# State-token block: first layer in three fp32r passes, low parts and convolution reordered, last stores cut in four

## The chip, the cores and the metric

One core of one Trainium2 chip runs the whole kernel. The metric is device time in microseconds (us) of one execution. The time before is the median of three runs, 946.2 us (944.11, 946.2 and 946.27).

## The reference, cut to what matters

Three layers follow one another. An attention reads `x` (8 batches, 8 heads, 512 tokens, 64 wide) against 32 state tokens and back, so that each batch has 512 + 32 tokens of width 512. Then a normalised two-layer block with a residual, then a gated causal convolution:

```python
xn = (x - mu) / np.sqrt(var + 1e-06) * g_ln
x  = x + np.maximum(xn @ w_ch1, 0.0) @ w_ch2      # 512 -> 2048 -> 512

gate_pre = sum(conv_w[k] * xp[:, k:k + S, :] for k in range(5))   # xp: x padded by 4 tokens in front
gate = 1.0 / (1.0 + np.exp(-gate_pre))
out  = (gate * (x @ w_val)) @ w_out
```

All arithmetic is float32.

## The kernel before, in words

**Arithmetic.** A float32 product is mostly made of three fp32r passes: each operand is split into a high part (a copy rounded to fp32r, made on ScalarE) and a low part (source minus high, made on VectorE or GpSimd), and `mm3` (lines 76 to 79) adds high by low, low by high and high by high. In the profile, L77, L78 and L79 are these three matmuls, whoever calls them. `split_sb` (lines 72 to 74) makes the two parts: L73 is the high one, L74 the low one.

**Stages.** The 512 ordinary tokens of batches 0 to 7 go through the two-layer block as token blocks b = 0 to 7. The 8 x 32 = 256 state tokens of all batches form one more token block, b = B = 8 ("the state block" below). Its input is made by `sread_block_steps` while block 7 runs: `xc` is the centred input, `xn` (line 420) is `xc` times the norm's weight `g`. `segment` (lines 536 to 629) runs 16 hidden slices f of 128 units: layer 1 into a PSUM tile `h`, relu into `hid` (L580 ScalarE high part, L582 VectorE low part), and layer 2, which for slice f is issued one slice later (`second`, by `run_pending`), so that TensorE goes L1(f), L2(f-1), L1(f+1), L2(f). For the ordinary blocks layer 1 is `mm3`. For the state block it is a plain float32 matmul, L565: four of them (k) per slice, 256 columns each, with the decoded weight pairs `w1_0` to `w1_7` as the stationary operand.

**The last stage.** For each of the nine blocks i, `split_x2` splits the block's result `x2` into high (L642) and low (L646 VectorE for i = 0, L644 GpSimd otherwise), `gate_x2` makes the convolution (L656, then four taps L658 on VectorE, then the sigmoid L670), `val_steps` multiplies by `w_val` and by the gate (L691) and splits the product, and `out_steps` multiplies by `w_out`, copies from PSUM (L707) and stores: two token tiles in one transfer (L711) for i < B, one transfer of 128 rows for each of the two tiles of the state block (L709). On TensorE the order is val(0), val(1), out(0), val(2), out(1), and so on to out(8). Each val uses the same four accumulators acc0 to acc3, so val(1) cannot begin slice e before L691 has read slice e of val(0).

**What sets the order.** TensorE's order is written out by hand. On the other engines a planner orders the instructions by priority and by a simulated timeline, and the engine then takes them in that fixed order. `behind` (lines 440 to 446) adds an ordering to that plan without a wait: the instruction comes after a marked one on the same engine. `marks["dve"]` is the last L582 of `segment`, `marks["act"]` the last L580. Behind the state block, in the slots after each slice (`before_phase_b`), run the loads of x2 of blocks 0 and 1, the decode of `w_out` (raw data go into the tiles `w1_0` to `w1_3`, once layer 1 has finished with these), and split and convolution of block 0.

**Buffers.** The tags `m` (two buffers, used by `m_steps` before), `ahl` (two) and `big` (two) are shared. x2 of block 1 takes a `big` buffer when the one before it is free.

Of the kernel before, what the change touches and what calls it, by code (L numbers as in the profile page):

```python
# [9 lines left out]
F32 = mybir.dt.float32  # L10
F32R = mybir.dt.float32r
# [4 lines left out]
AF = mybir.ActivationFunctionType  # L16
ALU = mybir.AluOpType
# [4 lines left out]
P = 128  # L22
# [22 lines left out]
def tile_kernel(ctx: ExitStack, tc: tile.TileContext, xT, xk, stT, sn, w1, w2, wval, wout, convw, gln, ident, out):  # L45
# [9 lines left out]
    def sb(shape, dt, tag, bufs=1):  # L55
        cnt[0] += 1
        return main.tile(shape, dt, tag=tag, bufs=BUFS.get(tag, bufs), name=f"{tag}_{cnt[0]}")
# [23 lines left out]
    def at_prio(p):  # L81
        tc.cur_priority = p
# [323 lines left out]
    def sread_block_steps():  # L406
        xs = sb([P, KT, NTS], F32, "big")
        for k in range(KT):
            nc.sync.dma_start(out=xs[:, k].rearrange("p (b n) -> p b n", n=NS), in_=x1d[:, :, k, :].rearrange("b p n -> p b n"))
        yield  # L410
        mu = at_ps([P, NTS])
        for k in range(KT):
            nc.tensor.matmul(mu, lhsT=nmean.to_broadcast([P, P]), rhs=xs[:, k], start=k == 0, stop=k == KT - 1)
        xc = sb([P, KT, NTS], F32, "big")
        xn = sb([P, KT, NTS], F32, "ahl")
        for k in range(KT):
            nc.vector.tensor_tensor(xc[:, k], xs[:, k], mu, op=ALU.add)
        yield
        for k in range(KT):
            nc.scalar.activation(xn[:, k], xc[:, k], AF.Copy, scale=g_sb[:, k])  # L420
        xns[B] = xn
        x1s[B] = xs
        yield
        sq = [t2([P, 2, NTS]) for _ in range(2)]
        for i in range(2):
            nc.scalar.activation(sq[i], xc[:, 2 * i:2 * i + 2], AF.Square)
        nc.gpsimd.tensor_tensor(sq[0], sq[0], sq[1], op=ALU.add)
        rstd_of(B, [sq[0][:, 0], sq[0][:, 1]], NTS)
        yield
# [102 lines left out]

    cs_done = set()
    clock = [BASE]

    def segment(b, f0, f1, n, nxt, bg):
        accs = {}
        for f in range(f0, f1):
            base = clock[0]
            clock[0] += 1000  # L540
            at_prio(base - DLEAD)
            for _ in range(next(share[0], 0)):
                next(slots[0], None)
            q, cols = f // QF, slice((f % QF) * P, (f % QF + 1) * P)
            unit = (b, q + 1) if (q + 1) * QF < f1 else nxt
            fresh = b < B and unit is not None and unit[1] not in cs_done
            if b < B and unit is not None and f % QF == 1 and not fresh:
                at_prio(base - 1500)
                m_steps(*unit)
            at_prio(base - HLEAD)  # L550
            if f == 1 and 1 < b < B:
                x1_group(b)
            at_prio(base)
            h = ps(ps_mm, "mm", [P, n])
            if b < B:
                m = ms[b, q]
                for u in range(2):
                    if plain(b, f):
                        nc.tensor.matmul(h, lhsT=m[:, u, 0, cols], rhs=aTs[b][:, u], start=u == 0, stop=u == 1)
                        continue  # L560
                    ahl = ahls[b]
                    mm3(h, m[:, u, 0, cols], m[:, u, 1, cols], ahl[:, u, 0], ahl[:, u, 1], u == 0, u == 1)
            else:
                for k in range(KT):
                    nc.tensor.matmul(  # L565
                        h, lhsT=w1s[4 * q + k][:, cols], rhs=xns[b][:, k], start=k == 0, stop=k == KT - 1
                    )
            if fresh and f % QF == 3:
                at_prio(base - 1500)
                colsum(unit[1])  # L570
                m_steps(*unit)
            if f == 1 and 1 < b < B:
                x1_mean(b)
            if f == f1 - 1:
                at_prio(base + LATE)
                for _ in bg:
                    pass
            at_prio(base - HLEAD)
            hid = sb([P, 2, n], F32 if plain(b, f) else F32R, "hid")
            marks["act"] = nc.scalar.activation(hid[:, 0], h, AF.Relu)  # L580
            if not plain(b, f):
                marks["dve"] = nc.vector.scalar_tensor_tensor(  # L582
                    hid[:, 1], h, 0.0, hid[:, 0].bitcast(F32), op0=ALU.max, op1=ALU.subtract
                )
            at_prio(base + 200)
            run_pending()

            def second(f=f, hid=hid):
                rrow = rstd_row(b, n) if f == f1 - 1 else None
                for d in range(KT):  # L590
                    if f == f0:
                        accs[d] = ps(ps_acc, f"acc{d}", [P, n])
                    cols = slice(d * P, (d + 1) * P)
                    if plain(b, f):
                        nc.tensor.matmul(accs[d], lhsT=plain_w2[f][:, cols], rhs=hid[:, 0], start=f == f0, stop=f == f1 - 1)  # L595
                    else:
                        mm3(accs[d], w2s[f][:, 0, cols], w2s[f][:, 1, cols], hid[:, 0], hid[:, 1], f == f0, f == f1 - 1)
                    if f == f1 - 1:
                        x1 = x1s[b]
                        dst = x1[:, d, :]  # L600
                        if b == B:
                            xp = sb([P, B, PAD + NS], F32, f"w1_{4 + d}")
                            nc.gpsimd.tensor_copy(xp[:, :, :PAD], halos[0][:, d])
                            x2s[B].append(xp)
                            dst = xp[:, :, PAD:]
                        t = t2([P, n])
                        p = tc.cur_priority
                        at_prio(p - HLEAD)
                        marks["dve"] = nc.vector.tensor_tensor(t, accs[d], rrow, op=ALU.mult)
                        at_prio(p)  # L610
                        eng = nc.vector if b < 2 or b >= B - 1 else nc.gpsimd
                        eng.tensor_tensor(dst, grouped(b, t), grouped(b, x1[:, d, :]), op=ALU.add)
                if f == NF - 1 and b < B:
                    nc.sync.dma_start(out=x2d[b], in_=x1s[b])
                    if not halos:
                        halos.append(sb([P, KT, B, PAD], F32, "halo"))
                    nc.gpsimd.tensor_copy(halos[0][:, :, b, :], x1s[b][:, :, S - PAD:])

            pend[0] = second
            at_prio(base + 500)  # L620
            next(bg, None)
# [15 lines left out]
    def split_x2(i, k):  # L637
        n = ntok(i)
        hl = sb([P, 2, n], F32R, f"w2_{4 * (i % 2) + k}")
        src = x2s[i][:, k] if i < B else x2s[i][k][:, :, PAD:]  # L640
        hi, lo = grouped(i, hl[:, 0]), grouped(i, hl[:, 1])
        behind(nc.scalar.activation(hi, src, AF.Copy), "act")  # L642
        if i:
            nc.gpsimd.tensor_tensor(lo, src, hi.bitcast(F32), op=ALU.subtract)  # L644
        else:
            behind(nc.vector.tensor_tensor(lo, src, hi.bitcast(F32), op=ALU.subtract), "dve")  # L646
        x2hl.setdefault(i, []).append(hl)
# [24 lines left out]
    def x2_steps(i):  # L672
        if i > B:
            return
        for k in range(KT):
            split_x2(i, k)
            yield
            gate_x2(i, k)
            yield

    def val_steps(i):
        n = ntok(i)
        hls = x2hl.pop(i)
        gt = gates.pop(i)
        gvs[i] = []
        for e in range(KT):
            v = ps(ps_acc, f"acc{e}", [P, n])
            cols = slice(e * P, (e + 1) * P)
            for k in range(KT):
                mm3(v, wv[k][:, 0, cols], wv[k][:, 1, cols], hls[k][:, 0], hls[k][:, 1], k == 0, k == KT - 1)  # L690
            nc.vector.tensor_tensor(gt[:, e], gt[:, e], v, op=ALU.mult)  # L691
            hl = sb([P, 2, n], F32R, f"w2_{8 + 4 * (i % 2) + e}")
            split_sb(hl[:, 0], hl[:, 1], gt[:, e], nc.vector)
            gvs[i].append(hl)
            yield

    def out_steps(i):
        n = ntok(i)
        hls = gvs.pop(i)
        for t in range(n // P):  # L700
# [5 lines left out]
                ob = sb([P, 2, DM], F32, "hid", 2)  # L706
            nc.scalar.copy(ob[:, t % 2], o)  # L707
            if i == B:
                nc.sync.dma_start(out=out[4 * t:4 * t + 4, S:, :], in_=ob[:, t % 2])  # L709
            elif t % 2:  # L710
                nc.sync.dma_start(  # L711
                    out=out[i, (t - 1) * P:(t + 1) * P, :].rearrange("(u p) d -> p u d", p=P), in_=ob
                )
# [249 lines left out]
```

## Time and profile before

| | us |
|---|---|
| median of three runs | 946.2 |
| profiled execution, its own time | 944.02 |
| its span, first to last instruction | 942.2 |
| TensorE busy in the span | 911.7 (97%) |
| VectorE busy | 563.9 (60%) |
| ScalarE busy | 367.4 (39%) |
| GpSimd busy | 193.1 (20%) |
| granted TensorE clock, mean share of full | 0.992 |

The profiled execution lasted 944.02 us, of which 942.2 lie between its first and its last instruction. A start time in a timeline is us from the beginning of the span. A matmul's duration is longer than the step to the next one, because matmuls are pipelined: the step between starts is what a matmul costs. In the same way the step between back-to-back VectorE instructions is a little shorter than the duration of one. The state block lies from 687 to 744 us, the last stage from 744 to the end.

### The profile page before, as it was taken

How to read it: one execution, taken by the hardware profiler on the slowest of the kernel's cores; microseconds unless marked ns; L12 is line 12 of the kernel's file. 1: busy time of each engine (PE TensorE's matmuls, PEld its weight loads, DVE VectorE, ACT ScalarE, POOL GpSimd, SP SyncE). 2: the span in 40 equal slices, each digit the busy share in tenths (PEclk: the TensorE clock that was granted, in tenths of full speed). 3: DMA queues.
4: the chain of work that ended last, by engine and by line, in shares of the span. 5: the costliest groups of instructions: out<-in, count | busy, mean ns of one | idle time of the engine just before them, and what ended most of it. 6: DMA issues, size and time to landing. Idle time of an engine off the chain costs nothing.

```text
span 942.2 us, 12810 instructions
## 1 busy us (share of the span) xinstructions
PE 911.7 (97%) x5087; PEld 687.9 (73%) x5088; DVE 563.9 (60%) x972; ACT 367.4 (39%) x672; POOL 193.1 (20%) x167
## 2 busy tenths in 40 slices
PE   7979999999999999999999999999999989999996
PEld 2327666777777777777777777777888878888884
DVE  6887997575357472453436336242138899988830
ACT  4646654233144332332314233232125454655521
POOL 0000000012114521412411241142102243232100
PEclk9989999999999999999999999999999999999999
DMA  9832220022103111111100110110021212321112
GB/s 364 325 114 93 71 71 1 1 93 96 41 8 118 46 48 48 48 48 49 48 21 25 48 45 1 27 46 18 27 90 46 90 45 90 129 96 62 51 67 67
DMA packets 26548, 66.45 MB, mean 71 GB/s; under 512 B 10744, under 2 KB 12920, under 8 KB 22392
## 3 DMA queue, kind: packets, MB, share of 16 engines
q1 hardware_dynamic: 26056, 64.45, 19.2%
q10 hardware_dynamic: 432, 1.18, 0.3%
q8 instruction: 40, 0.66, 0.3%
q14 instruction: 20, 0.16, 0.1%
HBM read 47.80 MB, written 17.83 MB: 70 GB/s over the span
## 4 chain that ended last, share of the span: by engine, by line
PE 79%; DVE 14%; DMA 2%; ACT 2%; issue 1%; SPq 0%; ACTq 0%; DVEq 0%
PE acc L77 14%; PE acc L79 14%; PE acc L78 13%; PE mm L77 8%; PE mm L79 7%; PE mm L78 7%; PE at L138 3%; DVE ahl L658 3%; PE at L77 2%; PE at L79 2%; PE at L78 2%; PE mm L565 1%; PE acc L595 1%; DVE w L458 1%; DVE hid L582 1%
## 5 line engine op out<-in xcount | busy, mean ns | idle before, releaser
L582 DVE SCALAR_TENSOR_TENSOR hid<-mm,hid 128x512 fp32r<-128x512 f32 (+1 forms) x140 | 92.2, 658 | 223.6 <-ACT hid L580 223.4
L77 PE MATMUL acc<-hid,w 128*128 128x512 f32 (+1 forms) x560 | 215.7, 385 | 2.3 <-DVE hid L582 1.2
L79 PE MATMUL acc<-hid,w 128*128 128x512 f32 (+1 forms) x560 | 211.5, 378 | 0.0
L78 PE MATMUL acc<-hid,w 128*128 128x512 f32 (+1 forms) x560 | 211.2, 377 | 0.0
L580 ACT ACTIVATE hid<-mm 128x512 fp32r<-128x512 f32 (+2 forms) x144 | 82.4, 572 | 246.8 <-PE mm L79 226.8
L77 PEld LDWEIGHTS acc<-hid,w 128*128 128x128 f32 x560 | 105.3, 188 | 25.4 <-DVE hid L582 2.2
L79 PEld LDWEIGHTS acc<-hid,w 128*128 128x128 f32 x560 | 105.3, 188 | 20.0
L78 PEld LDWEIGHTS acc<-hid,w 128*128 128x128 f32 x560 | 105.4, 188 | 19.4
L74 POOL TENSOR_TENSOR m<-mb,m 128x512 fp32r<-128x512 f32 x48 | 65.5, 1379 | 202.0 <-ACT m L73 202.0
L77 PE MATMUL mm<-ahl,m 128*128 128x512 f32 x248 | 102.3, 413 | 0.0
L658 DVE SCALAR_TENSOR_TENSOR ahl<-big,cw,ahl 128x509 f32<-128x509 f32 (+3 forms) x128 | 99.4, 830 | 4.1 <-ACT ahl L656 3.7
L78 PE MATMUL mm<-ahl,m 128*128 128x512 f32 x248 | 96.8, 390 | 0.2 <-DVE m L74 0.2
L79 PE MATMUL mm<-ahl,m 128*128 128x512 f32 x248 | 96.9, 391 | 0.0
L77 PEld LDWEIGHTS mm<-ahl,m 128*128 128x128 f32 x248 | 46.5, 188 | 38.0 <-issue 30.0
L73 ACT ACTIVATE m<-mb 128x512 fp32r<-128x512 f32 x62 | 39.1, 630 | 89.8 <-DVE mb L144 89.7
L644 POOL TENSOR_TENSOR w<-big,w 128x512 fp32r<-128x512 f32 x28 | 44.2, 1605 | 82.0 <-ACT w L642 82.0
L144 DVE SCALAR_TENSOR_TENSOR mb<-cs,sbn,at 128x512 f32<-128x512 f32 x62 | 43.5, 742 | 28.3 <-PE at L138 28.3
L77 PE MATMUL acc<-w,raw 128*128 128x512 f32 (+1 forms) x144 | 54.6, 379 | 2.5 <-DVE ahl L691 2.5
L78 PE MATMUL acc<-w,raw 128*128 128x512 f32 (+1 forms) x144 | 54.4, 378 | 0.0
L79 PE MATMUL acc<-w,raw 128*128 128x512 f32 (+1 forms) x144 | 54.3, 377 | 0.0
L79 PEld LDWEIGHTS mm<-ahl,m 128*128 128x128 f32 x248 | 46.5, 188 | 10.1
L78 PEld LDWEIGHTS mm<-ahl,m 128*128 128x128 f32 x248 | 46.7, 188 | 8.5 <-DVE m L74 0.5
(172 smaller groups left out, 1353.3 us busy)
## 6 DMA issues: line engine op xcount, KB each, us to landing
raw<-in_w SPq DMA_DIRECT2D x16, 512.0 KB, 4.7
w<-in_w SPq DMA_DIRECT2D x16, 512.0 KB, 9.8
big<-in_xk SPq DMA_DIRECT2D x8, 1024.0 KB, 4.9
x2d<-x SPq DMA_DIRECT2D x8, 1024.0 KB, 3.8
big<-x2d SPq DMA_DIRECT2D x8, 1024.0 KB, 4.9
out<-hid SPq DMA_DIRECT2D x16, 512.0 KB, 2.8
big<-in_xT SPq DMA_DIRECT2D x7, 1024.0 KB, 4.8
raw<-in_wval SPq DMA_DIRECT2D x4, 512.0 KB, 3.5
```

What stands on the lines that cost most here:

```text
L73: nc.scalar.activation(hi, src, AF.Copy)
L74: eng.tensor_tensor(lo, src, hi.bitcast(F32), op=ALU.subtract)
L77: nc.tensor.matmul(acc, lhsT=wh, rhs=xl, start=first, stop=False)
L78: nc.tensor.matmul(acc, lhsT=wl, rhs=xh, start=False, stop=False)
L79: nc.tensor.matmul(acc, lhsT=wh, rhs=xh, start=False, stop=last)
L138: nc.tensor.matmul(mp[u][32 * p:32 * p + 32, :], lhsT=stg[r, p, :], rhs=w1s[4 * q + p][r], start=True, stop=True)
L144: a = nc.vector.scalar_tensor_tensor(mb, cs[:, q], sbn[:, u], mp[u], op0=ALU.mult, op1=ALU.add)
L458: a = nc.vector.tensor_scalar(h[:, :, 0, 1], h[:, :, 1, 1], 0x8000, 0x4000, op0=ALU.bitwise_and, op1=ALU.bitwise_or)
L580: marks["act"] = nc.scalar.activation(hid[:, 0], h, AF.Relu)
L582: marks["dve"] = nc.vector.scalar_tensor_tensor(hid[:, 1], h, 0.0, hid[:, 0].bitcast(F32), op0=ALU.max, op1=ALU.subtract)
L644: nc.gpsimd.tensor_tensor(lo, src, hi.bitcast(F32), op=ALU.subtract)
L658: t = nc.vector.scalar_tensor_tensor(g[:, j:], x[:, :n - j], cw_sb[:, k, PAD - j:TAPS - j], g[:, j:], op0=ALU.mult, op1=ALU.add)
```

## The change

1. The state block's layer 1 becomes three fp32r passes. `xn` gets a high and a low part, and a new function `split_w1` splits the weights for two hidden slices at a time, in `m` buffers, two slices ahead of their use.
2. The low part of x2 of block 1 goes from GpSimd to VectorE, behind the last marked VectorE instruction. For block 1 all four splits come ahead of all four convolutions.
3. In `val_steps` the low part of the product becomes the new mark `marks["dve"]`, so convolutions emitted later are ordered behind it (for all blocks below B).
4. Each of the two last stores (256 KB, 128 rows) becomes four stores of 32 rows, on SyncE's and ScalarE's queues in turn.

```diff
@@ sread_block_steps
-        xn = sb([P, KT, NTS], F32, "ahl")
+        xn = sb([P, 2, KT, NTS], F32R, "ahl")
@@
-            nc.scalar.activation(xn[:, k], xc[:, k], AF.Copy, scale=g_sb[:, k])
+            nc.scalar.activation(xn[:, 0, k], xc[:, k], AF.Copy, scale=g_sb[:, k])
+            nc.vector.scalar_tensor_tensor(
+                xn[:, 1, k], xc[:, k], g_sb[:, k], xn[:, 0, k].bitcast(F32), op0=ALU.mult, op1=ALU.subtract
+            )
@@
+    w1hl = {}
+
+    def split_w1(i):
+        hl = sb([P, 2, KT, 2 * P], F32R, "m")
+        q, c = i // 2, slice((i % 2) * 2 * P, (i % 2 + 1) * 2 * P)
+        for j in range(2):
+            w = w1s[2 * q + j, "pair"][:, :, c]
+            split_sb(hl[:, 0, 2 * j:2 * j + 2], hl[:, 1, 2 * j:2 * j + 2], w, nc.vector)
+        w1hl[i] = hl
@@ segment
             at_prio(base - HLEAD)
+            if b == B and f % 2 == 0:
+                if f == 0:
+                    split_w1(0)
+                if f + 2 < f1:
+                    split_w1(f // 2 + 1)
@@
+                wc = slice((f % 2) * P, (f % 2 + 1) * P)
+                w, xn = w1hl[f // 2], xns[b]
                 for k in range(KT):
-                    nc.tensor.matmul(
-                        h, lhsT=w1s[4 * q + k][:, cols], rhs=xns[b][:, k], start=k == 0, stop=k == KT - 1
-                    )
+                    mm3(h, w[:, 0, k, wc], w[:, 1, k, wc], xn[:, 0, k], xn[:, 1, k], k == 0, k == KT - 1)
@@ split_x2
-        if i:
+        if i > 1:
             nc.gpsimd.tensor_tensor(lo, src, hi.bitcast(F32), op=ALU.subtract)
@@ x2_steps
             split_x2(i, k)
             yield
-            gate_x2(i, k)
-            yield
+            if i != 1:
+                gate_x2(i, k)
+                yield
+        if i == 1:
+            for k in range(KT):
+                gate_x2(i, k)
+                yield
@@ val_steps
-            split_sb(hl[:, 0], hl[:, 1], gt[:, e], nc.vector)
+            nc.scalar.activation(hl[:, 0], gt[:, e], AF.Copy)
+            a = nc.vector.tensor_tensor(hl[:, 1], gt[:, e], hl[:, 0].bitcast(F32), op=ALU.subtract)
+            marks["dve"] = a
@@ out_steps
             if i == B:
-                nc.sync.dma_start(out=out[4 * t:4 * t + 4, S:, :], in_=ob[:, t % 2])
+                for j in range(4):
+                    eng = nc.scalar if j % 2 else nc.sync
+                    eng.dma_start(out=out[4 * t + j, S:, :], in_=ob[32 * j:32 * j + 32, t % 2])
```

## Rows read from the trace of the kernel before

**Rows 1.** The page: busy time, share of the span and instructions of each engine.
```profile
PE 911.7 (97%) x5087; PEld 687.9 (73%) x5088; DVE 563.9 (60%) x972; ACT 367.4 (39%) x672; POOL 193.1 (20%) x167
```
**Rows 2.** Busy time by stretch: one stretch, the state block's sum, the first last-stage stretch.
```profile
711.00:726.00 15.00, 15.00 (x96) 13.82 (x95) 12.02 (x20) 8.71 (x16) 2.26 (x2) 1.00 0.19 70
...
sum 56.60, PE 55.40 PEld 50.67 DVE 36.74 ACT 21.96 POOL 7.41; mean PE 13.85 PEld 12.67 DVE 9.19 ACT 5.49 POOL 1.85
...
743.80:766.00 22.20, 19.72 (x87) 15.69 (x86) 22.05 (x26) 9.97 (x18) 13.30 (x8) 1.00 0.14 48
```
**Rows 3.** The chain that ended last, 699 to 744 us: start, length, what.
```profile
699.30 1.73 PE mm L565 x8
702.46 1.73 PE mm L565 x8
...
712.83 3.51 DMA w<-in_wout
...
739.41 4.89 DMA big<-x2d
```
**Rows 4.** TensorE's timeline, layer 2 of one slice: two matmuls, nine steps apart.
```profile
701.10 0.28 PE L79 MATMUL acc<-hid,w 128*128 128x256 f32 x1
...
702.17 0.28 PE L79 MATMUL acc<-hid,w 128*128 128x256 f32 x1
```
**Rows 5.** TensorE's timeline: the layer-1 starts of three slices in a row.
```profile
724.42 1.89 PE L565 MATMUL mm<-ahl,w 128*128 128x256 f32 x8
...
728.11 1.89 PE L565 MATMUL mm<-ahl,w 128*128 128x256 f32 x8
...
732.48 1.89 PE L565 MATMUL mm<-ahl,w 128*128 128x256 f32 x8
```
**Rows 6.** TensorE's waits from 686 us to the end: total us, times, longest.
```profile
PE acc L77 <- DVE ahl L691: 2.5, 2, 1.5
PE acc L77 <- DVE hid L582: 1.2, 2, 0.9
```
**Rows 7.** VectorE's and GpSimd's timelines: convolution taps alone, and beside GpSimd's low parts.
```profile
731.07 2.32 DVE L658 SCALAR_TENSOR_TENSOR ahl<-big,cw,ahl 128x511 f32<-128x511 f32 x3 [0.18 <-ACT ahl L656]
...
745.60 1.55 DVE L658 SCALAR_TENSOR_TENSOR ahl<-big,cw,ahl 128x511 f32<-128x511 f32 x1
...
748.52 3.48 DVE L658 SCALAR_TENSOR_TENSOR ahl<-big,cw,ahl 128x511 f32<-128x511 f32 x2
...
745.03 6.41 POOL L644 TENSOR_TENSOR w<-big,w 128x512 fp32r<-128x512 f32 x4 [4.07 <-ACT w L642]
```
**Rows 8.** Groups by line and shape: the two halves of a split, 512 elements.
```profile
L73 ACT ACTIVATE m<-mb 128x512 fp32r<-128x512 f32 x62 | 39.1, 630 | 89.8 <-DVE mb L144 89.7
...
L74 DVE TENSOR_TENSOR m<-mb,m 128x512 fp32r<-128x512 f32 x14 | 9.5, 688 | 0.1
```
**Rows 9.** ScalarE's and VectorE's timelines: relu and low part of one slice.
```profile
697.90 0.39 ACT L580 ACTIVATE hid<-mm 128x256 fp32r<-128x256 f32 x1 [2.77 <-PE mm L565]
...
698.32 0.42 DVE L582 SCALAR_TENSOR_TENSOR hid<-mm,hid 128x256 fp32r<-128x256 f32 x1 [2.07 <-ACT hid L580]
```
**Rows 10.** The end: last copy, last store's issue, SyncE's wait for it.
```profile
933.19 0.59 ACT L707 COPY hid<-mm 128x512 f32<-128x512 f32 x1 [2.09 <-PE mm L79]
...
933.80 0.54 SPq L709 DMA_DIRECT2D out<-hid  x1
...
SPq L959 <- DMA out<-hid: 6.8, 1, 6.8
```
**Rows 11.** DMA packets, 931.5 to 941.5 us: the two last stores alone.
```profile
DMA packets 264, 0.52 MB, mean 52 GB/s; under 512 B 8, under 2 KB 8, under 8 KB 264
```
**Rows 12.** DMA packets, 906 to 909 us: one store of 512 KB alone.
```profile
DMA packets 272, 0.52 MB, mean 175 GB/s; under 512 B 16, under 2 KB 16, under 8 KB 272
```
**Rows 13.** DMA issues: transfer, count, KB each, median us from issue to landing.
```profile
out<-hid SPq DMA_DIRECT2D x16, 512.0 KB, 2.8
...
x1d<-t SPq DMA_DIRECT2D x32, 16.0 KB, 3.7
```

## The prediction

> **What bounds the kernel now.** I read the page first. TensorE is busy for 97% of the span [rows 1], so what the change can win lies in three places: less TensorE work, the few waits that TensorE has, and the tail in which it has none. VectorE's 60% is an average; it says nothing of the stages that the change touches. So I looked at busy time by stretch. In the 56.6 us of the state block VectorE is busy for 36.7 us, but 12.0 of 15 in one stretch of it, and in the first 22.2 us of the last stage for 22.05 [rows 2]. There VectorE is as much the bound as TensorE.
>
> The chain says the same: through the first slices of the state block it runs in TensorE's L565 and its layer 2, then leaves TensorE at a load of `w_out` at 712.8 and later at the load of x2 of block 1 at 739.4 [rows 3], with VectorE and ScalarE work between. The waits tell what that costs. From 686 us on TensorE waits 1.2 us for `hid` and 2.5 us for L691, and for nothing else that the view shows [rows 6]. Behind the second of these the remaining blocks run without a wait, so a gain made before them reaches the end undiminished. The last thing is the store: the last copy ends at 933.78, and SyncE then waits 6.8 us for the transfer [rows 10].
>
> **Layer 1 of the state block.** The eight float32 instructions of a slice cost 1.73 us, the whole slice 3.16 us (702.46 less 699.30) [rows 3]. Layer 2 of the same 256 columns is already what layer 1 becomes: nine fp32r steps in 1.07 us, 0.119 each, so twelve cost 1.43 [rows 4]. The two sum to the 3.16. After the change a slice is 2 x 1.43 = 2.86, and sixteen of them save 16 x 0.30 = **4.8 us** of TensorE time.
>
> What that buys is paid on other engines. `split_w1` adds two high and two low parts per pair of slices, of 512 elements, sixteen of each. A high part takes 0.63 us on ScalarE, a low part 0.69 on VectorE [rows 8]. ScalarE gets 10 us, in a block where it is busy for 22.0 of 56.6 [rows 2]: hidden. VectorE gets 16 x 0.69 = 11.0, of which the first split (1.4) can run ahead of the block, since its buffer is free before block 7 ends. The other 9.6 make 46.3 us of VectorE work. Without its waits the block takes 56.6 - 4.8 = 51.8 us; VectorE would be 89% busy. `xn`'s four low parts lie 30 us ahead of the block and cost nothing as long as they are there.
>
> **Waits inside the state block.** Three starts of layer 1 lie 3.69 and 4.37 us apart instead of 3.16 [rows 5], so 0.53 + 1.21 = 1.7 us are lost now to late `hid` tiles. Two things speak for less of it: the first parts of `w_out` may be loaded as soon as the splits have read the weight tiles, not when TensorE has, two or more slices sooner, so their decode moves into VectorE's quiet slices. One speaks for more: 9.6 us of new work, and a slice that is shorter by 0.3. The upper bound of the gain is 1.7, all waits gone. For the lower bound I take the stretch where TensorE stalls now, VectorE at 80%, as all it can do: 46.3 / 0.8 = 57.9 us, 1.3 longer than now, so that the 4.8 are lost too. I take 0, waits as they are, since every added split has its inputs early: its buffer is free after slice 2i-3 and it is needed at slice 2i, five half-slices or 5 x 1.43 = 7.2 us later, against 2.6 us for two high and two low parts one behind the other (0.63 and 0.69 each [rows 8]).
>
> **Block 1's low parts and the pinned convolution.** These two edits go together. Now the four low parts take GpSimd 6.41 us from 745.0, and VectorE's taps beside them take 1.55 us and 3.48 for two, against 2.32 for three alone [rows 7]. On VectorE four low parts cost 4 x 0.69 = 2.8 us [rows 8], and three taps get back some 1.5 to 2.7 us, so for VectorE this is about even. What matters is the order. Taps of block 1 now stand ahead of L691 of block 0, and val(1) waits for those to free its accumulators: 2.5 us in two waits [rows 6]. With the taps behind the low parts of val(0), L691 and its split come as soon as TensorE delivers a slice, every 2.7 us (12 steps of 19.72 / 87 = 0.227 [rows 2]), and the convolution fills the time of val(1). What is late next is the low part of x2 of block 1, which val(1) needs at once and which stands behind that of val(0)'s first and second slices. Its load starts when block 0's convolution ends, at 739.4, and takes 4.9 us [rows 3], so the data are there 0.5 us after val(0) begins at 743.8. Val(0)'s second slice is done 5.4 us after its beginning, its split some 2 us later, the last two low parts 1.4 behind: 8.8 of the 10.9 us that val(0) takes, 2 to spare. Gain **2.5 us**; bounds 0 (a new wait as long) and 2.5. Later blocks get the pin as well: VectorE idles a little while it waits for a val slice, but a finished accumulator is needed again only after val and out of a block (22 us), which hides it.
>
> **The last stores.** A store of 512 KB leaves 256 packets of 2 KB and 16 small ones [rows 12]; the two last stores together leave 256 and 8 [rows 11]. I read the small ones as one per DMA engine and transfer: 16 engines there, 4 here. The first destination is rows by columns, the last ones 4 x 32 x columns, and 4 fits the outer dimension. So the last store runs on a quarter of the engines, at 52 GB/s, behind the one before it. The pieces have 32 rows as their outer dimension and should spread over 16. Each queue issues two; an issue takes 0.54 [rows 10], and a store twice as big in all lands 2.8 us from its issue [rows 13]. So the end comes 0.5 + 2.8 = 3.3 us after the last copy, against 0.54 + 6.8 = 7.3: gain **4.0 us**. The bounds come from the landing time: 3.7, as the smallest transfers need [rows 13], gives 3.1; 1.4, if half the bytes took half the time, gives 5.4. ScalarE's two issues for the first tile stand ahead of its last copy, which comes 2.7 us later: hidden.
>
> **Sum.** 4.8 + 0 + 2.5 + 4.0 = 11.3 us. The profiled execution took 944.0, so the sum gives 932.7. The three runs lie 0.1 to 2.2 above that execution, and their median 2.2. I take 0.8 of it: 933.5.
>
> **Rivals.**
> *VectorE bounds the state block.* For it: VectorE 80% busy where TensorE stalls now, and 89% to come. Against: the quiet slices at the start, and `hid` and the splits have precedence in the plan. At 85% the block takes 46.3 / 0.85 = 54.5, a gain of 2.1 in place of 4.8: 944.0 - 2.1 - 2.5 - 4.0 = 935.4. At 80% it is 1.3 longer than now: 938.8.
>
> *The pieces don't land sooner.* If two pieces of a queue land one behind the other at the 3.7 us of the smallest transfers, the end comes 7.4 us after the last copy and the gain is 0: 936.7. For it: those transfers too come from 32 partitions. Against: four of them share a queue with other work, and their runs are far shorter. The Trainium skill has a rule for this side (SBUF — State Buffer, "Can I just issue two DMAs to hit both halves?"): transfers from different partition ranges serialise, and all ports are reached only by one transfer over all 128 partitions. By it the store's gain would be 0, too; no run here has shown such a pair yet.
>
> *Slower: a split behind a pinned convolution.* The convolution of block 0 is ordered behind L582 of slices 7, 9, 11 and 13. If the plan puts the low parts for slice 8, 10, 12 or 14 behind it, layer 1 waits: from the start of the relu 0.84 to the end of L582 [rows 9], four taps at 0.77 [rows 7], two low parts at 0.69 [rows 8], 5.3 us, of which layer 2 covers 1.43. That is 3.9 x 4 = 15.5 us: 944.0 - 11.3 + 15.5 = 948.2. It decides from 11.3 / 4 = 2.8 us per slice pair on. Against it: the split is ready and has precedence two slices before.
>
> *Nothing comes of it*, all lost in waits of this kind: 944.
>
> **How the numbers follow.** Chances: forecast 0.62, VectorE as the bound 0.22, stores without a gain 0.09, nothing 0.03, slower 0.04. A measurement of this kernel can tell about 0.3%, 2.8 us, from no change. The first three cases are faster by more than that: 0.93; same 0.03; slower 0.04. The range goes down to 929.5 (waits in the block gone and pieces at the better bound, 944.0 - 4.8 - 1.7 - 2.5 - 5.4 = 929.6) and up to 940.5, VectorE at 80% with the scatter of the runs on it.
>
> **What would show it.** Right: slices 2.86 us apart, L565 gone, twelve more rows of L77 to L79 per slice; no wait for L691 near 755; eight small stores spread over 16 engines, the last landing 3 us behind the last copy. Wrong: slices over 3.1 us apart with waits for a split's L74 or for L582; a wait of val(1) for L74 of block 1; SyncE waiting over 5 us at the end.

## The result, and the profile after

The changed kernel takes 932.93 us (median of four runs, 931.7 to 933.91), against 945.15 of the kernel before beside it: a ratio of 0.9876, 95% interval 0.9862 to 0.989, so 12.2 us less by the medians. The forecast was 933.5 in a range of 929.5 to 940.5. The profiled execution took 931.7 us, 12.3 less than that of before.

Line numbers have moved: L582 is now L599 (low part of `hid`), L580 L597, L658 L675 (taps), L646 L663 (block 1's low part, now VectorE), L691 L713, L707 L731 (last copy), L709 L735 (last stores), L609 L626 (the end of a block); layer 1 of the state block is in L77 to L79.

Where did the 12.3 us come from? The span is cut at four events that both timelines show: the first matmul of the state block, the first of val(0), the first of out(0), the end of the last copy (L707 or L731). The stretches, in us, for every kernel of this study, the experiments below among them:

| kernel | state block begins at | block, to val(0) | val(0) to out(0) | out(0) to last copy | last copy to end |
|---|---|---|---|---|---|
| before | 687.42 | 56.41 | 24.87 | 165.08 | 8.42 |
| changed | 687.43 | 52.34 | 21.78 | 165.07 | 3.28 |
| changed, again | 687.76 | 52.64 | 21.78 | 165.07 | 3.25 |
| 1 layer 1 alone | 688.62 | 52.51 | 24.38 | 165.06 | 8.33 |
| 2 order alone | 691.04 | 56.40 | 22.50 | 165.06 | 8.20 |
| 3 stores alone | 688.37 | 56.40 | 24.89 | 165.08 | 3.26 |
| 4 pieces on one queue | 689.57 | 52.66 | 21.78 | 165.07 | 3.92 |
| 5 pieces of 2 x 32 rows | 688.13 | 52.69 | 21.78 | 165.06 | 12.64 |
| 6 no mark in val | 690.39 | 52.35 | 21.78 | 165.07 | 3.31 |
| 7 block 1's low parts on GpSimd | 688.97 | 52.40 | 21.78 | 165.07 | 3.28 |
| 8 late decode | 687.63 | 52.73 | 23.46 | 165.07 | 3.31 |
| 9 late decode, ordered copy | 689.12 | 50.16 | 21.77 | 165.08 | 3.27 |
| 11 splits first, nothing else of 2 and 3 | 687.34 | 52.83 | 24.41 | 165.07 | 3.25 |
| 12 splits in turn | 687.98 | 53.93 | 33.08 | 165.08 | 3.33 |

Without a wait in it, val(0) to out(0) repeats to 0.01 us, out(0) to the last copy to 0.02, and the end to 0.1 with the pieces on two queues, 0.2 without. The block varies by 0.5 us where TensorE's program in it is the same: 52.34 to 52.83 in the two executions of the changed kernel and in experiments 1, 4 to 7 and 11. The changed kernel run again lies 0.3 above its first execution, where its expectation (below) allowed 0.2. The rest of what differs lies ahead of the state block, where no kernel here differs on TensorE: it begins between 687.3 and 691.0, and over the first 60 us the granted clock lies between 0.88 and 0.92 in these executions. So the effects below are read from the stretches, and the medians of runs stand beside them. Experiments 4 to 7, 11 and 12 have a single execution each, whose whole time can't tell effects of 3 us apart. The changed kernel has won 4.1 us in the block, 3.1 between val(0) and out(0) and 5.1 after the last copy; nothing elsewhere.

The page, for comparison with [rows 1]:

```profile
PE 906.5 (97%) x5152; PEld 687.2 (74%) x5152; DVE 578.5 (62%) x996; ACT 375.4 (40%) x688; POOL 191.9 (21%) x163
```

TensorE is as full as before; it simply has less to do. VectorE has 14.6 us more and ScalarE 8.0 us more, in a shorter span.

**The block.** TensorE's timeline, the first layer-1 matmul of slices 1, 2, 7 and 8, and the one wait between the last two:

```profile
692.53 0.28 PE L77 MATMUL mm<-ahl,m 128*128 128x256 f32 x1
...
695.41 0.28 PE L77 MATMUL mm<-ahl,m 128*128 128x256 f32 x1
...
709.80 0.28 PE L77 MATMUL mm<-ahl,m 128*128 128x256 f32 x1
...
713.15 0.39 PE L77 MATMUL acc<-hid,w 128*128 128x256 f32 x1 [1.75 <-DVE hid L599]
...
714.69 0.28 PE L77 MATMUL mm<-ahl,m 128*128 128x256 f32 x1
```

A slice takes 2.88 us (695.41 less 692.53), where it took 3.16 [rows 3]. One slice takes 4.89, 2.0 more, because a `hid` tile comes late. It is TensorE's only wait from the state block to the end (total us, times, longest); the two groups of [rows 6] have become one:

```profile
PE acc L77 <- DVE hid L599: 1.7, 1, 1.7
```

The busy times of the block, to be held against the sum in [rows 2] (columns: length, then TensorE, weight loads, VectorE, ScalarE, GpSimd with counts, clock, DMA share, GB/s):

```profile
687.00:739.80 52.80, 51.05 (x412) 50.12 (x411) 44.51 (x76) 27.95 (x55) 8.77 (x9) 1.00 0.22 81
```

VectorE is busy for 84% of it. The chain that ended last says why the tile at 713 is late; these are its pieces from 699.9 us (start, length, what):

```profile
699.93 0.39 ACT hid L597
700.31 0.53 ACT m L73
700.86 0.70 DVE m L74
701.58 4.02 DMA w<-in_wout
705.69 0.69 ACT w L453
706.39 0.76 DVE w L461
...
709.50 1.28 DVE m L74 x2
710.78 1.74 DVE w L461
...
712.76 0.34 DVE hid L599
713.15 0.39 PE acc L77
```

Low part of a weight split (L74), then the load of the third and fourth part of `w_out` into the tiles that the split has just read, then ScalarE's decode (L453) as soon as the data have landed. ScalarE stood in front of it, with the relu of slice 5 behind it in its queue. That relu begins at 707.35 and the next one, of slice 6, at 710.32; ScalarE works without a pause in between. ScalarE's waits in the block:

```profile
ACT w L453 <- DMA w<-in_wout: 2.4, 1, 2.4
```

The last part of the chain is VectorE's. The relu of slice 6 is done at 710.7, but the low part that TensorE waits for (L599) begins only at 712.68, behind a weight split and a step of the decode (L461). That step takes 1.82 us here and 0.75 or 0.76 the other three times in the block; beside it GpSimd makes a low part of `w_out`. VectorE's timeline, then GpSimd's:

```profile
710.70 1.82 DVE L461 TENSOR_SCALAR w<-w 128x512 uint16<-128x512 uint16 x1
...
712.68 0.41 DVE L599 SCALAR_TENSOR_TENSOR hid<-mm,hid 128x256 fp32r<-128x256 f32 x1
...
710.49 1.42 POOL L74 TENSOR_TENSOR w<-c,w 128x512 fp32r<-128x512 f32 x1 [1.47 <-ACT w L73]
```

So the late tile has two candidates, ScalarE's stand and VectorE's slow step.

**The tail.** The timelines of ScalarE and of the two queues at the end, against [rows 10]:

```profile
926.03 0.59 ACT L731 COPY hid<-mm 128x512 f32<-128x512 f32 x1 [2.09 <-PE mm L79]
...
926.64 0.78 SPq L735 DMA_DIRECT2D out<-hid  x2
926.65 0.85 ACTq L735 DMA_DIRECT2D out<-hid  x2
```

The queue's own waits (total us, times, longest):

```profile
SPq L985 <- DMA out<-hid: 1.4, 2, 1.2
```

The copy ends at 926.62, both queues issue two pieces at once, and behind the last issue SyncE waits 1.4 us where it waited 6.8. Another 1.1 us pass from there to the end of the span, as before. DMA packets and issues from 922 us on, against [rows 11 to 13]:

```profile
DMA packets 656, 1.05 MB, mean 140 GB/s; under 512 B 144, under 2 KB 144, under 8 KB 656
...
out<-hid SPq DMA_DIRECT2D x4, 64.0 KB, 1.7
out<-hid ACTq DMA_DIRECT2D x4, 64.0 KB, 2.0
```

In this window lie one store of 512 KB (16 small packets [rows 12]) and eight pieces: the other 128 small packets make 16 per piece. I read that as 16 engines for every piece; experiment 5 tries this reading. The median from issue to landing is 1.7 us on SyncE's queue and 2.0 on ScalarE's.

### The profile page after: what moved, and what is told of

It is laid out like the page before. It is cut to its first block, busy times and chain, and to the rows that moved or that the text cites. A ratio compares the mean times of both kernels' runs of the same rounds, so it can differ in the third digit from the quotient of the medians.

```text
span 929.9 us, 12963 instructions
## 1 busy us (share of the span) xinstructions
PE 906.5 (97%) x5152; PEld 687.2 (74%) x5152; DVE 578.5 (62%) x996; ACT 375.4 (40%) x688; POOL 191.9 (21%) x163
## 4 chain that ended last, share of the span: by engine, by line
PE 86%; DVE 9%; ACT 2%; DMA 2%; issue 1%; ACTq 0%; DVEq 0%; SPq 0%
PE acc L77 15%; PE acc L79 15%; PE acc L78 15%; PE mm L77 8%; PE mm L79 8%; PE mm L78 8%; PE at L138 4%; PE at L77 2%; PE at L79 2%; PE at L78 2%; PE acc L612 1%; PE mm L885 1%; DVE w L461 1%; DVE hid L599 1%; DMA big<-in_xT 1%
## 5 line engine op out<-in xcount | busy, mean ns | idle before, releaser
L599 DVE SCALAR_TENSOR_TENSOR hid<-mm,hid 128x512 fp32r<-128x512 f32 (+1 forms) x140 | 92.1, 658 | 211.1 <-ACT hid L597 210.9
L77 PE MATMUL acc<-hid,w 128*128 128x512 f32 (+1 forms) x560 | 213.4, 381 | 2.8 <-DVE hid L599 1.7
L79 PE MATMUL acc<-hid,w 128*128 128x512 f32 (+1 forms) x560 | 211.5, 378 | 0.0
L597 ACT ACTIVATE hid<-mm 128x512 fp32r<-128x512 f32 (+2 forms) x144 | 82.5, 573 | 245.8 <-PE mm L79 243.2
L77 PEld LDWEIGHTS acc<-hid,w 128*128 128x128 f32 x560 | 105.4, 188 | 25.1 <-DVE hid L599 2.1
L77 PE MATMUL mm<-ahl,m 128*128 128x512 f32 (+1 forms) x312 | 120.4, 386 | 0.0
L79 PEld LDWEIGHTS acc<-hid,w 128*128 128x128 f32 x560 | 105.4, 188 | 20.0
L78 PE MATMUL mm<-ahl,m 128*128 128x512 f32 (+1 forms) x312 | 114.9, 368 | 0.2 <-DVE m L74 0.2
L79 PE MATMUL mm<-ahl,m 128*128 128x512 f32 (+1 forms) x312 | 115.1, 369 | 0.0
L74 POOL TENSOR_TENSOR m<-mb,m 128x512 fp32r<-128x512 f32 x48 | 65.3, 1375 | 202.0 <-ACT m L73 202.0
L675 DVE SCALAR_TENSOR_TENSOR ahl<-big,cw,ahl 128x511 f32<-128x511 f32 (+3 forms) x128 | 104.3, 860 | 0.4
L77 PEld LDWEIGHTS mm<-ahl,m 128*128 128x128 f32 x312 | 58.8, 188 | 38.1 <-issue 30.0
L79 PEld LDWEIGHTS mm<-ahl,m 128*128 128x128 f32 x312 | 58.8, 189 | 10.1
L78 PEld LDWEIGHTS mm<-ahl,m 128*128 128x128 f32 x312 | 59.0, 189 | 8.6 <-DVE m L74 0.5
L661 POOL TENSOR_TENSOR w<-big,w 128x512 fp32r<-128x512 f32 x24 | 38.5, 1632 | 92.7 <-ACT w L659 76.8
L79 PE MATMUL acc<-w,raw 128*128 128x512 f32 (+1 forms) x144 | 54.3, 377 | 0.0
L77 PE MATMUL acc<-w,raw 128*128 128x512 f32 (+1 forms) x144 | 54.3, 377 | 0.0
```

Source lines behind the costliest of these rows:

```text
L74: eng.tensor_tensor(lo, src, hi.bitcast(F32), op=ALU.subtract)
L77: nc.tensor.matmul(acc, lhsT=wh, rhs=xl, start=first, stop=False)
L78: nc.tensor.matmul(acc, lhsT=wl, rhs=xh, start=False, stop=False)
L79: nc.tensor.matmul(acc, lhsT=wh, rhs=xh, start=False, stop=last)
L599: marks["dve"] = nc.vector.scalar_tensor_tensor(hid[:, 1], h, 0.0, hid[:, 0].bitcast(F32), op0=ALU.max, op1=ALU.subtract)
L675: t = nc.vector.scalar_tensor_tensor(g[:, j:], x[:, :n - j], cw_sb[:, k, PAD - j:TAPS - j], g[:, j:], op0=ALU.mult, op1=ALU.add)
```

## The experiments

### The parts one by one

Three kernels are the kernel before with one part of the change each. Experiment 1 has the hunks of `sread_block_steps` and `segment` and `split_w1`:

```diff
+    def split_w1(i):
...
-                        h, lhsT=w1s[4 * q + k][:, cols], rhs=xns[b][:, k], start=k == 0, stop=k == KT - 1
+                    mm3(h, w[:, 0, k, wc], w[:, 1, k, wc], xn[:, 0, k], xn[:, 1, k], k == 0, k == KT - 1)
```

> Only the first part of the change: layer 1 of the state block in three passes, the rest as before. Theory (the parts are independent): val(0) begins 4.1 us sooner, as in the changed kernel (743.8 to about 739.8 in the trace), the 2.5 us of waits for L691 stay, the tail after the last copy stays at 8.4 us; the time falls by about 4 us (ratio 0.996). Rival (VectorE sets the pace up to 766 us, so the gain is given back to it): val(0) begins sooner but the waits for L691 grow to 5 us or more, and the time falls by under 2 us (ratio 0.998 to 1.000).

Measured: ratio 0.9954 (0.9936 to 0.9972), median 940.92. The block takes 52.51 us, 3.9 less than before, and val(0) to out(0) 24.38, 0.5 less. TensorE's waits from the block on:

```profile
PE acc L77 <- DVE ahl L708: 2.0, 2, 1.0
PE acc L77 <- DVE hid L599: 1.8, 1, 1.8
```

L708 is here the product with the gate (L691 before): 2.0 us instead of 2.5. The gain of the block is not given back. The theory holds, with the waits for the product 0.5 us shorter than it said, and the wait of 1.8 us for `hid` comes with layer 1 alone.

Experiment 2 has the hunks of `split_x2`, `x2_steps` and `val_steps`:

```diff
-        if i:
+        if i > 1:
             nc.gpsimd.tensor_tensor(lo, src, hi.bitcast(F32), op=ALU.subtract)
...
+        if i == 1:
+            for k in range(KT):
+                gate_x2(i, k)
...
+            marks["dve"] = a
```

> Only the second and third part: the low parts of block 1 on VectorE, its splits ahead of its convolutions, and the convolutions behind the low parts of val; layer 1 in float32 and the stores whole. Theory: val(0) begins at 743.8 as before, no wait for L691 is left, the last copy ends 3 us sooner, the time falls by about 3 us (ratio 0.997). Rival (the waits went because layer 1 released VectorE's decode sooner, not because of the order): waits for L691 or for a low part of 1 us or more stay and the time falls by under 1.5 us.

Measured: ratio 0.9984 (0.9973 to 0.9995), median 943.19. The block is unchanged at 56.40, and val(0) to out(0) takes 22.50, 2.4 less. The waits:

```profile
PE acc L77 <- DVE hid L582: 1.2, 2, 0.9
PE acc L77 <- DVE w L646: 0.4, 1, 0.4
```

No wait for the product with the gate is left: that came from the order. A new one has appeared, 0.4 us for the low part of block 1, which is what the prediction named as late next; with the faster layer 1 it is gone. So 2.4 of the 3.1 us belong to the order alone, and the rest needs layer 1 as well. The whole time fell by 1.5 us only (0.5 to 2.5 by the interval), where 3 were expected; the stretches do not show where the rest went, which leaves the part ahead of the state block.

Experiment 3 has the four pieces on two queues:

```diff
-                nc.sync.dma_start(out=out[4 * t:4 * t + 4, S:, :], in_=ob[:, t % 2])
+                for j in range(4):
+                    eng = nc.scalar if j % 2 else nc.sync
+                    eng.dma_start(out=out[4 * t + j, S:, :], in_=ob[32 * j:32 * j + 32, t % 2])
```

> Only the fourth part: the last stores in four pieces on two queues. Theory: all as before up to the last copy, then 3.3 us to the end of the span instead of 8.4; the time falls by 5 us (ratio 0.995). Rival (the tail is shorter in the changed kernel because other transfers lie elsewhere): the tail falls by under 3 us.

Measured: ratio 0.9969 (0.9957 to 0.9981), median 942.11. All stretches are those of before but the last, 3.26 us instead of 8.42: 5.2 us from the stores alone. (The ratio of the runs shows 3 us of it; the state block of the profiled execution began 1.0 us later than before.) By the stretches the three parts add up: 3.9 + 0.5, 2.4 and 5.2 make 12.0, the whole change 12.3. By the ratios of whole runs they make 8.8 us (4.3, 1.5 and 2.9), against 11.7 for the whole change; each interval is 1 to 2 us wide to either side, and what lies ahead of the block is not explained.

### Why the pieces land sooner

Experiment 4 leaves the pieces and takes the second queue away:

```diff
-                    eng = nc.scalar if j % 2 else nc.sync
+                    eng = nc.sync
```

> The changed kernel with all four pieces on SyncE's queue. Theory (what helped is that a piece spreads over 16 engines): two more issues of 0.4 us come in a row, the tail after the last copy is 3.3 + 0.8 = 4.1 us. Rival (two queues are what helped): over 6 us.

Measured: 3.92 us after the last copy. The second queue is worth 0.6 us: the four issues on one queue end 1.75 us after the copy, those on two queues 0.8. The pieces on a single queue already have 4.5 of the 5.1.

Experiment 5 makes two pieces, each with the destination 2 x 32 rows x columns:

```diff
-                for j in range(4):
+                for j in range(2):
                     eng = nc.scalar if j % 2 else nc.sync
-                    eng.dma_start(out=out[4 * t + j, S:, :], in_=ob[32 * j:32 * j + 32, t % 2])
+                    eng.dma_start(out=out[4 * t + 2 * j:4 * t + 2 * j + 2, S:, :], in_=ob[64 * j:64 * j + 64, t % 2])
```

> The changed kernel with each last store in two pieces of 2 x 32 rows, one per queue. Theory (the number of engines is that of the outer dimension, so two per piece, and the lowest ones each time): 2 small packets per piece, the engines that carry them are fewer than with the one store of 4 x 32 rows, the tail after the last copy is 8.4 us or more, some 12. Rival (what helped is two queues and smaller pieces): about 4 us.

Measured: 12.64 us after the last copy, 4.2 more than the uncut store, although the pieces are smaller and on two queues. SyncE's wait:

```profile
SPq L985 <- DMA out<-hid: 11.1, 2, 9.8
```

The packets of the last 12 us:

```profile
DMA packets 236, 0.47 MB, mean 39 GB/s; under 512 B 8, under 2 KB 8, under 8 KB 236
```

Eight small packets for four pieces, two each. The busy share of the 16 DMA engines is a second witness. Each row cuts its window into 40 slices, one digit a slice, in tenths: first the kernel before from 931.5 us on, then the two pieces of this experiment, then the kernel changed from 922 us on, where the first group of 9s is the store of 512 KB and the last two groups are the eight pieces:

```profile
DMA  0000341301222222222330323131222111100000
...
DMA  1100111101111111111111111111111110000000
...
DMA  5999999700000009997970000000088979700000
```

Two engines of 16 would be 0.13, four 0.25. The pieces of this experiment stay at 0.1 although both queues have one under way, so both use the same two engines. The uncut stores lie mostly at 0.1 to 0.3, and the pieces of 32 rows reach 0.9. Together with [rows 11] this settles it. An outer dimension of 2 gave 2 engines and 39 GB/s, one of 4 gave 4 engines and 52 GB/s, and one of 32 gave 16 engines and a landing after 1.7 to 2.0 us. The Trainium skill states this rule (DMA: Bandwidth & Descriptors, "Why a DMA increments its semaphore by 16 and not by 1"): the largest number up to 16 that divides the slowest dimension of both sides, dimensions of size 1 left out. The runs agree in all three cases.

### What the order needs

Three edits work together in val: splits ahead of convolutions, low parts on VectorE, the mark. Experiments 6, 7 and 12 each take one away from the changed kernel, 11 takes two.

```diff
 # 6
-            marks["dve"] = a
 # 7
-        if i > 1:
+        if i:
 # 12
-            if i != 1:
-                gate_x2(i, k)
-                yield
-        if i == 1:
-            for k in range(KT):
-                gate_x2(i, k)
-                yield
+            gate_x2(i, k)
+            yield
```

> The changed kernel without the new mark in val_steps, so that the convolutions of blocks 1 to 7 are ordered by the planner alone. Theory (the order behind the low parts of val is what removed the waits for the product with the gate): waits of TensorE for it, or for the low parts, come back, val(0) to out(0) takes 23 to 25 us instead of 21.8. Rival (moving block 1's splits ahead and to VectorE is enough): 21.8, no wait.

> The changed kernel with the low parts of block 1 on GpSimd again. Theory: GpSimd's four parts take 6 us or more beside VectorE's work, the last comes some 7 us after the data have landed, about when val(1) begins; val(0) to out(0) takes 21.8 to 22.5 us. Rival (the two engines' sharing is what cost the 2.5 us): 23.5 us or more, with waits for VectorE.

Both give 21.78 us with no wait in val. Experiment 6 is a miss: I had held the mark to be what removed the waits. Experiment 7 gave the time expected, but I had the low parts later and slower than they are. On GpSimd they take 5.32 us here (6.41 before [rows 7]); none of VectorE's taps run beside them now:

```profile
742.77 5.32 POOL L661 TENSOR_TENSOR w<-big,w 128x512 fp32r<-128x512 f32 x4 [12.30 <-ACT w L659]
```

They are done at 748.1, and val(1) begins some 10.9 us after val(0), at 752.3, 4 us later. So neither edit is needed beside the other. Is either?

> The changed kernel without the mark in val_steps and with block 1's low parts on GpSimd; of the second and third part only the order of block 1's four splits ahead of its four convolutions is left. Theory (mark and VectorE's low parts are each enough by itself beside the splits first, but one of them is needed): waits for the product with the gate come back, val(0) to out(0) takes 23 us or more. Rival (the splits first are what counts): 21.8, no wait.

Measured: 24.41 us, and the wait of before is back:

```profile
PE acc L77 <- DVE ahl L713: 2.0, 2, 1.7
```

With the splits first, one of the two is needed and each is enough. Without a mark and with GpSimd beside it, VectorE takes five taps ahead of the second L713, in 5.7 us where five alone would take 3.9 (by the three of [rows 7]).

> The changed kernel with block 1's splits and convolutions in turn, as before; mark and low parts on VectorE stay. Theory (the order of the splits is a necessary part): val(1) waits for the last low part of block 1, which stands behind three convolutions, val(0) to out(0) takes 23 us or more. Rival (the mark alone does it): 21.8, no wait.

Measured: 33.08 us from val(0) to out(0), 11.3 more than the changed kernel, the costliest edit of the study. TensorE's waits:

```profile
PE acc L77 <- DVE w L663: 7.3, 2, 5.8
```

Val(1) waits for the third and fourth low part of block 1, which VectorE reaches late, the third behind five taps of the first two groups. Four of these five ran beside GpSimd's low parts of block 2 and took 1.15 to 1.8 us each, against 0.77 alone [rows 7]:

```profile
759.39 0.68 DVE L663 TENSOR_TENSOR w<-big,w 128x512 fp32r<-128x512 f32 x1
...
762.57 0.68 DVE L663 TENSOR_TENSOR w<-big,w 128x512 fp32r<-128x512 f32 x1
```

With the mark and VectorE's low parts, the splits first are a necessity: without them the stretch takes 8.2 us more than in the kernel before. The mark alone, or the low parts alone, in the kernel before was not run. The 11.3 us are more than the 7.3 of waiting; the clock has the rest (last section).

### The wait that is left

The theory of the chain above: ScalarE stands at a decode whose load has not landed, and the relu behind it comes late. Experiment 8 decodes the last two parts of `w_out` behind the convolution of block 0:

```diff
-        yield from prep_weights(wout, wo, [f"w1_{k}" for k in range(KT)])
-        yield from x2_steps(0)
+        decode = prep_weights(wout, wo, [f"w1_{k}" for k in range(KT)])
+        for _ in range(2):
+            next(decode)
+            yield
+        yield from x2_steps(0)
+        yield from decode
```

> The changed kernel with the decode of the second two parts of the output weights moved behind the split and convolution of block 0, which move two slices ahead. Theory (the 1.75 us that TensorE still waits for a hidden tile come from ScalarE standing 2.4 us at a decode whose load has not landed): that wait is gone, val(0) begins about 2 us sooner than in the changed kernel, at some 737.8, and the time is 930.9, some 2 us below the changed kernel's 932.9. Rival (VectorE, 84% busy in the block, is what is short): waits for hidden tiles of 1.5 us or more turn up at other slices and the time is that of the changed kernel within 0.5 us.

Measured: ratio 0.9901 (0.9884 to 0.9918), median 935.04, no better than the changed kernel, where some 2 us less were expected. The wait for `hid` is gone, but another of 2.4 us stands ahead of val(0):

```profile
PE acc L77 <- DVE t L626: 2.4, 1, 2.4
```

The rival expected something like it, for another reason: VectorE short of time. But VectorE is idle then. ScalarE's timeline shows the planner's new order, splits and first taps of block 1 ahead of the copy L378, on which the end of the state block (L626) depends:

```profile
734.96 2.18 ACT L659 ACTIVATE w<-big 128x512 fp32r<-128x512 f32 x4
737.04 2.54 ACT L673 ACTIVATE ahl<-big,cw 128x512 f32<-128x512 f32 x4
739.49 0.35 ACT L378 COPY t<-at 128x256 f32<-128x256 f32 x1
```

Experiment 9 orders them behind that copy, by the mark that they already follow:

```diff
-        nc.scalar.copy(r, rrow)
+        a = nc.scalar.copy(r, rrow)
+        if key == B:
+            marks["act"] = a
```

> The run with the late decode, and ScalarE's splits of block 1 ordered behind its copy of the state block's norm row, which stood behind them there and held val(0) up for 2.4 us. Theory: both waits are gone; from the first matmul of the state block to val(0) 50.2 us (52.3 in the changed kernel), from val(0) to out(0) 21.8, the rest as in the changed kernel; the time 2.1 us below that of the changed kernel run beside it. Rival (VectorE's load is what is short): one of the two stretches stays 1.5 us or more longer than that, with a wait for VectorE in it.

> The changed kernel once more, beside the run before it. Theory: stretch lengths as before (52.3 to val(0), 21.8 to out(0), 3.3 after the last copy), each within 0.2 us; what differs between executions lies ahead of the state block.

Measured: the block takes 50.16 us, val(0) to out(0) 21.77, and TensorE has no wait from the state block to the end. The median is 930.67 us (ratio 0.9857, 0.9839 to 0.9876) beside 933.67 of the changed kernel on the same chip (0.9892, 0.9876 to 0.9908). It beats both kernels; against the changed one the intervals just touch, and the block, 2.2 us below the shortest of the others, is the clearer sign. Its VectorE is busy for 84% of the block, as in the changed kernel:

```profile
689.10:739.28 50.18, 50.18 (x410) 49.64 (x408) 42.15 (x76) 28.78 (x57) 8.79 (x9) 1.00 0.23 85
```

So VectorE at 84% of the block is no bound; the order in the queues was what cost time. Two things went together, though: with the late decode ScalarE no longer stands at a load, and the step L461 (L463 in experiment 9) takes 0.75 to 0.77 us each time, in experiments 8 and 9. Which of the two cost TensorE its 1.75 us no experiment separates. The 2.4 us of experiment 8 were ScalarE's order, as experiment 9 shows.

## Why the prediction was right, step by step

**Layer 1: right.** 2.86 us were predicted for a slice, 2.88 measured; sixteen of them give 4.5 us, 4.8 were forecast. That a matmul of the same shape costs the same in another place was the whole argument, and it carried.

**Waits in the block: near in size by luck, the reason right only in part.** I took the 1.7 us of waits as unchanged; they are 2.2 now (2.0 in slice 7, 0.2 in slice 9). These are not the waits of before left standing: those came later in the block, from 724 us on [rows 5]. The step that failed is the choice of the engine. I bounded the waits by VectorE's load, and named the earlier load of `w_out` as what speaks for less. It did come earlier, its second pair at 701.6 instead of 712.8 [rows 3], but the planner put ScalarE's decode earlier still, and so ScalarE stood at it with relus behind, and VectorE's step beside GpSimd was slow on top. TensorE never waits for a weight split itself, as I had argued, though two of them stand in the chain ahead of the late tile (709.50). The rival had VectorE as the bound at 85% and a block of 54.5 us; it took 52.3, and experiment 9 shows VectorE as busy with no wait on TensorE.

**The order: right in sign and size, too broad in its reasons.** Forecast 2.5, measured 3.1. Of the 0.6 more, half is in the count of the waits: before, the two steps with a wait in them took 1.87 and 1.39 us, 2.8 more than two plain steps of 0.227, where the view counts 2.5. The other half lies in the steps behind, 0.33 and 0.34 us for the first and some 0.24 for several after the first wait. That the move to VectorE is "about even" for it is what experiment 7 shows: VectorE is busy for 18.2 us from val(0) to out(0) with the low parts, 18.1 without. That what matters is the order was right, but of the mark I said more than it does: with the low parts on VectorE and the splits first the planner finds a good order by itself. The margin of val(1) was predicted as 2 us. The last low part ends at 749.7, and val(1) begins at 750.7: 1 us. Experiment 12 and the 0.4 us of experiment 2 show what happens without a margin.

**The stores: right in mechanism, mis-sized.** Forecast 4.0, measured 5.1. The term at fault is the landing time: I took the 2.8 us of a store of 512 KB, and pieces of 64 KB land in 1.7 to 2.0, nearer the better bound of 1.4. That the end came 3.3 us after the last copy, as forecast, is luck: 1.1 us pass between SyncE's wait and the end of the span, in both kernels, and I had left them out of both sums. They make 8.4 of my 7.3 before, and after the change they make up for a landing that I had 0.8 to 1.1 us too long. The rival that pieces gain nothing had the Trainium skill's rule beside it, that transfers from different partition ranges serialise (SBUF — State Buffer, "Can I just issue two DMAs to hit both halves?"). Here it does not decide the time: four pieces of 32 partitions on a single queue end 3.9 us after the last copy, where the whole store took 8.4.

**The slower rival** had its place right in kind: a part that TensorE needs, queued behind taps on VectorE. It did not come for the weight splits, which had precedence; experiment 12 shows that it costs 11 us for block 1's splits.

**The sum** came nearer than its terms: layer 1 was 0.3 us too high and the waits 0.5, the order 0.6 too low and the stores 1.1, so that 11.3 stand against 12.2.

## What to carry to other kernels

When a store or load is slow, look at its small packets and at the busy share of the DMA engines: in the three cases here they told how many engines carried it, and the outer dimension of the access pattern set that number. When a wait remains, follow the chain past the engine that TensorE names, piece by piece: a decode ahead of its data held up the relus behind it in the same queue, and a step on VectorE took 1.82 us instead of 0.75 beside GpSimd. And when several ordering edits come together, take each away in turn; here the splits first were needed beside the other two, and those two could stand in for each other.

## What the runs showed of the hardware

**The same wait cost more in one execution than in others.** In the changed kernel TensorE idles 1.75 us ahead of 713.15 and the next matmuls step at 0.12 us; in experiment 12 it idles 1.75 us at the same slice, up to 713.97, and the granted clock from 715 to 720 us is 0.71, with steps of 0.21 up to 717.8. That block took 53.93 us instead of 52.3 to 52.8, and nothing in its code up to there differs on TensorE. In the eight other executions with this wait, the changed kernel's among them, the clock is 1.00 over the 5 us behind it. After the longer idle times below it fell both times: after 2.4 us in experiment 8 (first two lines) it was 0.50 for 3.1 us, the 1.2 GHz level, and after 5.8 us in experiment 12 it was 0.50 for 9.5 us, in which TensorE waited 1.5 us more. Columns as in the block's windows above; first experiment 8:

```profile
738.00:740.40 2.40, 0.04 (x1) 0.05 (x1) 0.52 (x2) 1.84 (x4) 0.00 (x0) 0.98 0.01 3
740.40:743.50 3.10, 3.10 (x7) 2.44 (x8) 2.23 (x7) 0.00 (x0) 0.00 (x0) 0.50 0.00 0
```

Then experiment 12, behind the wait of 1.75 us and behind the one of 5.8:

```profile
715.00:720.00 5.00, 5.00 (x33) 5.00 (x33) 4.96 (x8) 1.53 (x3) 2.46 (x3) 0.71 0.00 0
...
759.50:769.00 9.50, 7.35 (x16) 5.30 (x17) 9.50 (x15) 4.87 (x8) 0.00 (x0) 0.50 0.00 0
```

So the longer waits cost 1.5 to 1.7 times their length: 11.3 us for 7.3 in experiment 12, and 1.7 us on top of the 2.4 in experiment 8. Why the 1.75 us did so once and not at other times was not tried. **A transfer over fewer engines** is the other surprise in size: cutting the last store into two made the tail 4.2 us longer than not cutting it.
